# One step for two attention products: the next block's values and the following block's scores are issued together on TensorE, and the values go into the PSUM pair of the next FF1 step

## The chip, the cores and the metric

The kernel runs on one core of one Trainium2 chip. The time is device microseconds of one execution, and the kernel before has a median of 899.84 us over three runs (899.83 to 900.71). Below, TensorE is the matrix engine (PE in the profile, with PEld for its weight loads), VectorE is DVE, ScalarE is ACT, and SyncE (SP) issues the DMAs. PSUM, the memory into which TensorE writes, is used here as four pairs of banks.

## The reference, cut to what matters

Attention inside chunks of 64 rows feeds a feed-forward layer with a rational activation. With 8 batches of 576 tokens there are 4608 tokens, of 8 heads with 64 columns each:

```python
scores = scale * np.matmul(q_c, k_c.transpose(0, 1, 2, 4, 3))
scores = scores - np.max(scores, axis=-1, keepdims=True)
attn = np.exp(scores)
attn = attn / (np.sum(attn, axis=-1, keepdims=True) + 1e-09)
out = np.matmul(attn, v_c)              # x: (4608, 512)
...
h = x @ w_in                            # (4608, 2048)
P = a[0] + a[1] * h + a[2] * h2 + a[3] * h3
Q = 1.0 + np.abs(b[0]) * np.abs(h) + np.abs(b[1]) * h2
g = P / (Q + 1e-06)
return (g @ w_out).astype(np.float32)   # (4608, 512)
```

Everything is float32. The feed-forward products are made from numbers split into a high and a low part, with three products in place of one.

## The kernel before, in words

The tokens are cut into 18 blocks of 256. Each block n has four **stages** s, one for each quarter of the 2048 hidden columns, and a pair (n, s) is a **step** g. Steps 0 to 11 stand in a table written by hand (START) that also splits the weights. From step 12 on, where block 3 begins, a loop writes the steps in one fixed order, and neither a scheduler nor a planner moves anything: the order of the code is the order of each engine's queue. A letter stands for one operation. On TensorE a step holds

- F and f, the first layer (FF1, L332), 48 matmuls of 128x256 into the PSUM tile ph, which lies in the pair p0 or p1 by turns (`ph_tag`);
- Z, z and y, the second layer (FF2, L407) of the step two before (`LAG`), into the pair po, which gathers the four stages of a block.

The rational function of a step runs on ScalarE (a, b and c read ph; I and J, the logarithm and the exponential, follow) and on VectorE (Q; p and P, which read ph; g, H, R, G). FF2 waits for the results of g and G, called ghi and glo. The next FF1 step in the same pair, two steps later, can begin only after P.

The attention of a later block m is laid between these:

- S, the scores (L205, `quarters`): 32 products of 64x64, which the profile shows as 64 matmuls, four at a time in the four quarters of the array, into pss; then M and U on VectorE (maximum, L241 and L249), E on ScalarE (16 exponentials with their sums, L260), n and N on VectorE (L269, L270, L275);
- T, eight transposes on TensorE (L284) into pst, and K, their copy on ScalarE (L288) into at;
- A, the values (L205 again): another 64 such matmuls, into psx; then X on ScalarE and Y on VectorE (L311, L315), which read psx and write the high and low part of the block's x, the input of F.

In the kernel before, pss, pst and psx all take the fourth pair, pa, one after the other. While block n runs, the attention of block m = n + 1 has S, M, U and E in stage 0, n and N in stage 1 with T and K at its end, and A, X and Y in stage 2. Stage 3 holds none of it. The first FF2 matmul after a block of `quarters` is cut at 280 columns instead of 256 (`CUT_FIRST`). SyncE loads q and k of a later block after S, and v after A; its queue also holds the stores of the output, which are issued in stage 1.

Of the kernel before, what the change touches and what calls it, by code (L numbers as in the profile page):

```python
# [19 lines left out]
NB = 18  # L20
# [26 lines left out]
FIRST = 12  # L47
# [7 lines left out]
def tile_chunked_attention_rational_moe(  # L55
# [32 lines left out]
    def bank_pair(tag, name):  # L88
        return ps.tile([P, 2, 512], F32, tag=tag, name=name)
# [4 lines left out]
    def load_qk(n, early=False):  # L94
        if n >= NB:
            return
        if early:
            q, k = (p2.tile([P, W], F32, tag=t, name=f"{t}qk{n}") for t in "AB")
        else:
            qk = p2.tile([P, 2, W], F32, tag="raw", name=f"qk{n}", bufs=3)  # L100
            q, k = qk[:, 0, :], qk[:, 1, :]
        loaded["q", n], loaded["k", n] = q, k
        if not early:
            load_part(n, slice(0, W))

    def load_part(n, c):
        for src, key in ((qT, "q"), (kT, "k")):
            nc.sync.dma_start(out=loaded[key, n][:, c], in_=src[n][:, c])

    def load_v(n):  # L110
        if n >= NB:
            return
        v = p2.tile([P, W], F32, tag="vt", name=f"v{n}", bufs=1)
        nc.sync.dma_start(out=v, in_=vP[n])
        loaded["v", n] = v
# [82 lines left out]
    def quarters(out_cols, tile_out, stat, mov, u):  # L198
        before[0] = "quarters"
        for g in range(NQ)[groups_of(u)]:  # L200
            for par in range(2):
                for c in range(2):
                    rows = slice(64 * c, 64 * c + 64)
                    cols = slice(g * 128 + par * 64, g * 128 + par * 64 + 64)
                    nc.tensor.matmul(  # L205
                        tile_out[par * 64:(par + 1) * 64, c, out_cols(g)],
                        stat[rows, cols], mov[rows, cols], start=True, stop=True,
                    )
# [4 lines left out]
    def have(key, n, make):  # L213
        if (key, n) not in att:
            att[key, n] = make()
        return att[key, n]
# [75 lines left out]
    def att_av(n, u=None, tag="pa"):  # L292
        psx = have("x", n, lambda: bank_pair(tag, f"psx{n}"))

        def cols(g):
            v, hp = divmod(g, NHP)
            return slice(hp * 128 + v * 64, hp * 128 + v * 64 + 64)

        quarters(cols, psx, loaded["v", n], att["at", n], u)
# [116 lines left out]
    def store(n):  # L416
        o = p2.tile([P, 2, DM], F32, tag="eo", name=f"o{n}")
        nc.scalar.copy(o, obuf.pop(n))
        for c in range(2):
            for u in range(UPB):  # L420
                nc.sync.dma_start(out=rows_out(n)[c, u], in_=o[64 * u:64 * u + 64, c, :])
# [3 lines left out]
    def ff2_end(n, s):  # L425
        ghi, glo = gbuf[n, s]
        for i in range(2):
            mm = [(g, w, fi) for g, w in ((ghi, wo_hi), (ghi, wo_lo), (glo, wo_hi)) for fi in range(FPS)]
            for k, (g, w, fi) in enumerate(mm):
                for c in (0, 1):  # L430
                    cols = slice(256 * c, 256 * c + 256)
                    nc.tensor.matmul(  # L432
                        accs[n][i][:, cols], g[:, fi, i * 128:(i + 1) * 128], w[:, FPS * s + fi, cols],
                        start=False, stop=(k == len(mm) - 1 and c == 1),
                    )
            o = p2.tile([P, DM], F32, tag="AB"[i], name=f"oe{i}")
            nc.scalar.copy(o, accs[n][i])
            for u, queue in ((0, nc.sync), (1, nc.scalar)):
                queue.dma_start(out=rows_out(n)[i, u], in_=o[64 * u:64 * u + 64, :])
# [3 lines left out]
    def ph_tag(g):  # L443
        return "p1" if g == 1 or (g >= 10 and g % 2 == 0) else "p0"
# [42 lines left out]
    def run(program, then=""):  # L487
        letters = [item[0] for item in program.split()] + [then]
        for k, item in enumerate(program.split()):
            ahead[0] = next((x for x in letters[k + 1:] if x in "FfZzyr"), "")  # L490
            do[item[0]](*map(int, item[1:].split(".")))
# [4 lines left out]
    total = len(steps)  # L496
    for g in range(FIRST, total + LAG):
        n, s = steps[min(g, total - 1)]
        m, stage = n + 1, s if n + 1 < NB and g < total else None
        one = lambda letters, k: run(" ".join(f"{x}{k}" for x in letters))  # L500
        if g < total:
            one("Ffab", g)
            if stage == 1:
                one("nN", m)
            one("cQ", g)
            if stage == 0:
                one("SMU", m)
                load_qk(m + 1)
            if stage == 2:
                one("A", m)  # L510
                load_v(m + 1)
            one("IJpP", g)
            if stage == 0:
                one("E", m)
            if stage == 2:
                one("X", m)
            one("gHRG", g)
            if stage == 2:
                one("Y", m)
        back = steps[g - LAG]  # L520
        if back == steps[-1]:
            ff2_end(*back)
            continue
        run(" ".join(f"{x}{g - LAG}" for x in "Zzy"), "F" if g + 1 < total else "Z")
        if back[1] == NST - 1:
            store(back[0])
        if stage == 1:
            one("TK", m)


# [34 lines left out]
```

## Time and profile before

| what | value |
|---|---|
| median of three runs | 899.84 us (899.83 to 900.71) |
| span of the profiled execution | 898.1 us |
| around it, to the median of the runs | 1.7 us |
| PE busy | 870.1 us, 97% |
| DVE busy | 748.0 us, 83% |
| ACT busy | 581.9 us, 65% |
| granted TensorE clock, mean | 0.996 |
| FF1 steps (L332) and FF2 (L407 into po) on the chain that ended last | 43% and 42% |
| scores (pss), values (psx), transposes (pst) on that chain | 2%, 2%, 2% |

The span runs from the first to the last instruction of one profiled execution, and the time of a run holds a little more than that. The last two rows are from the chain of waits, followed back from the last instruction. A PE that is 97% busy is not one at its peak, since matmuls are pipelined; how fast they follow each other is read from their starts.

### The profile page before, as it was taken

Reading aid. Unit: us, or ns where it says so; the run is one execution under the profiler, and the core shown is the slowest. Engines: PE = TensorE matmul, PEld = TensorE weight load, DVE = VectorE, ACT = ScalarE, POOL = GpSimd, SP = SyncE. Lnnn points to the kernel's source line nnn. Section 1 sums busy time; section 2 is a strip of 40 time slices with the busy share of each in tenths; the row PEclk is TensorE's granted clock in tenths of the full one; section 3 lists DMA queues with packets and bytes.
Section 4 is the critical chain, followed back from the end, with each engine's and each line's share of the span. In section 5 each row is a group of like instructions: output and inputs, shape, how many; then the busy total and the mean of one; then the engine's idle time right before and its main releaser. Section 6 shows DMA issues by size and latency. Waiting matters only on the chain.

```text
span 898.1 us, 21079 instructions
## 1 busy us (share of the span) xinstructions
PE 870.1 (97%) x9390; PEld 854.2 (95%) x9390; DVE 748.0 (83%) x671; ACT 581.9 (65%) x981; POOL 0.8 (0%) x8
## 2 busy tenths in 40 slices
PE   2699999999999999999999999999999999999998
PEld 2498999999999999999999999999999999999998
DVE  6999997898878878787878897878787878878784
ACT  6899987676656566665747475757565656566452
POOL 0000000000000000000000000000000000000000
PEclk9999999999999999999999999999999999999999
DMA  8525432103030303030201111020202030101010
GB/s 303 213 96 188 168 115 51 69 1 95 2 95 1 95 2 94 1 94 2 65 32 29 68 25 72 17 81 1 95 2 95 1 95 2 48 1 25 1 24 25
DMA packets 16506, 55.88 MB, mean 62 GB/s; under 512 B 2592, under 2 KB 2592, under 8 KB 14368
## 3 DMA queue, kind: packets, MB, share of 16 engines
q1 hardware_dynamic: 16256, 54.28, 18.5%
q8 instruction: 74, 1.21, 0.5%
q10 hardware_dynamic: 160, 0.26, 0.1%
q14 instruction: 16, 0.13, 0.0%
HBM read 45.09 MB, written 9.44 MB: 61 GB/s over the span
## 4 chain that ended last, share of the span: by engine, by line
PE 93%; DVE 3%; DMA 1%; ACT 1%; issue 1%; SPq 0%; ACTq 0%; DVEq 0%
PE ph L332 43%; PE po L407 42%; PE psx L205 2%; PE pss L205 2%; PE pst L284 2%; PE pe L407 1%; DMA Bqk<-in_kT 1%; PE pl L181 1%; DMA raw<-in_w_out 1%; DVE raw L165 0%; PE pe L432 0%; PE po L432 0%; DVE C L360 0%; DVE C L364 0%; DVE raw L161 0%
## 5 line engine op out<-in xcount | busy, mean ns | idle before, releaser
L332 PE MATMUL ph<-xhi,wi_hi 128*128 128x256 f32 x1152 | 322.7, 280 | 6.8 <-DVE C L364 6.8
L332 PE MATMUL ph<-xlo,wi_hi 128*128 128x256 f32 x1152 | 319.8, 278 | 0.0
L332 PE MATMUL ph<-xhi,wi_lo 128*128 128x256 f32 x1152 | 319.5, 277 | 0.0
L337 ACT ACTIVATE A<-ph,ab 128x1024 f32<-128x1024 f32 x72 | 80.7, 1121 | 253.9 <-PE ph L332 253.2
L332 PEld LDWEIGHTS ph<-xhi,wi_hi 128*128 128x128 f32 x1152 | 217.3, 189 | 8.3 <-ACT raw L153 7.5
L407 PE MATMUL po<-wo_hi,ghi 128*128 128x256 f32 (+1 forms) x1112 | 220.4, 280 | 0.0
L332 PEld LDWEIGHTS ph<-xlo,wi_hi 128*128 128x128 f32 x1152 | 217.7, 189 | 0.1
L332 PEld LDWEIGHTS ph<-xhi,wi_lo 128*128 128x128 f32 x1152 | 217.5, 189 | 0.0
L407 PE MATMUL po<-wo_lo,ghi 128*128 128x256 f32 x1112 | 217.1, 276 | 0.0
L348 DVE SCALAR_TENSOR_TENSOR B<-B,ab,A 128x1024 f32<-128x1024 f32 x72 | 92.4, 1283 | 99.0 <-ACT B L340 99.0
L407 PEld LDWEIGHTS po<-wo_hi,ghi 128*128 128x128 f32 x1112 | 167.6, 188 | 2.3 <-issue 0.3
L407 PEld LDWEIGHTS po<-wo_lo,ghi 128*128 128x128 f32 x1112 | 167.6, 188 | 0.0
L407 PE MATMUL po<-wo_hi,glo 128*128 128x256 f32 (+1 forms) x1112 | 138.1, 277 | 0.1
L407 PEld LDWEIGHTS po<-wo_hi,glo 128*128 128x128 f32 x1112 | 131.5, 188 | 0.3 <-DVE glo L381 0.3
L369 DVE SCALAR_TENSOR_TENSOR ghi<-C,ab,A 128x1024 fp32r<-128x1024 f32 x72 | 92.4, 1283 | 10.8 <-ACT A L356 2.4
L352 ACT ACTIVATE A<-B,cst 128x1024 f32<-128x1024 f32 x72 | 83.1, 1155 | 24.8 <-DVE B L348 24.7
L377 DVE SCALAR_TENSOR_TENSOR B<-C,ab,B 128x1024 f32<-128x1024 f32 x72 | 92.3, 1283 | 2.3
L364 DVE SCALAR_TENSOR_TENSOR C<-C,ab,ph 128x1024 f32<-128x1024 f32 x72 | 92.1, 1280 | 2.1
L381 DVE TENSOR_TENSOR glo<-B,A 128x1024 fp32r<-128x1024 f32 x72 | 88.2, 1224 | 6.6
L360 DVE TENSOR_TENSOR C<-C,ph 128x1024 f32<-128x1024 f32 x72 | 87.4, 1214 | 4.2 <-ACT B L340 3.6
L344 ACT ACTIVATE C<-ph,ab 128x1024 f32<-128x1024 f32 x72 | 87.6, 1216 | 4.5 <-PE ph L332 4.5
L373 DVE SCALAR_TENSOR_TENSOR B<-B,ghi 128x1024 f32<-128x1024 f32 x72 | 88.2, 1224 | 2.3
(72 smaller groups left out, 737.3 us busy)
## 6 DMA issues: line engine op xcount, KB each, us to landing
v<-in_vP SPq DMA_DIRECT2D x18, 512.0 KB, 4.1
out<-o SPq DMA_DIRECT2D x68, 128.0 KB, 2.4
raw<-in_w_in SPq DMA_DIRECT2D x8, 1024.0 KB, 6.1
raw<-in_w_out SPq DMA_DIRECT2D x8, 1024.0 KB, 4.8
qk<-in_qT SPq DMA_DIRECT2D x16, 512.0 KB, 4.8
qk<-in_kT SPq DMA_DIRECT2D x16, 512.0 KB, 5.6
Aqk<-in_qT SPq DMA_DIRECT2D x2, 256.0 KB, 5.3
Bqk<-in_kT SPq DMA_DIRECT2D x2, 256.0 KB, 5.8
```

The source lines that it names most:

```text
L332: nc.tensor.matmul(ph[:, fi, :], w[:, cc, f], x[:, cc, :], start=(k == 0), stop=(k == len(mm) - 1))
L337: nc.scalar.activation(ch[n, s][1], ch[n, s][0], AF.Abs, scale=b0)
L344: nc.scalar.activation(ch[n, s][3], ch[n, s][0], AF.Identity, bias=a2, scale=a3)
L348: nc.vector.scalar_tensor_tensor(B, B, b1a, A, ALU.mult, ALU.add)
L352: nc.scalar.activation(A, B, AF.Ln, bias=cst[:, 0:1], scale=2.0 ** -KLN)
L360: nc.vector.tensor_mul(C, C, h)
L364: nc.vector.scalar_tensor_tensor(C, C, a1, h, ALU.add, ALU.mult)
L369: nc.vector.scalar_tensor_tensor(gbuf[n, s][0], C, a0, A, ALU.add, ALU.mult)
L373: nc.vector.scalar_tensor_tensor(B, B, CQ, gbuf[n, s][0].bitcast(F32), ALU.add, ALU.mult)
L377: nc.vector.scalar_tensor_tensor(B, C, a0, B, ALU.add, ALU.subtract)
L381: nc.vector.tensor_mul(gbuf[n, s][1], B, A)
L407: nc.tensor.matmul(accs[n][i][:, cols], g[:, fi, i * 128:(i + 1) * 128], w[:, FPS * s + fi, cols], start=start, stop=stop,)
```

## The change

The loop's order changes, and nothing else does. S of block n + 2 (`early`) is now issued in stage 2 of block n, directly behind A of block n + 1; M, U and E of block n + 2 stand in stage 3, and n and N in stage 0 of the next block. T and K stay at the end of stage 1. A writes into the PSUM pair of the next FF1 step (`ph_tag(g + 1)`) instead of pa. X moves ahead of I on ScalarE, and Y between p and P on VectorE. In stage 2, q and k are loaded right behind v. At step 12 the first S of the loop still stands alone, with M, U, E, n and N where they were; the last A (block 17) stands alone too. Thirteen pairs lie between them (scores of blocks 5 to 17).

```diff
-        m, stage = n + 1, s if n + 1 < NB and g < total else None
+        stage = s if g < total else None
+        m = n + 1 if n + 1 < NB else None
+        early = n + 2 if n + 2 < NB else None
...
             one("Ffab", g)
-            if stage == 1:
+            if stage == 0 and m is not None and g > FIRST:
+                one("nN", m)
+            if g == FIRST + 1:
                 one("nN", m)
             one("cQ", g)
-            if stage == 0:
+            if g == FIRST:
                 one("SMU", m)
                 load_qk(m + 1)
-            if stage == 2:
-                one("A", m)
+            if stage == 3 and early is not None:
+                one("MU", early)
+            if stage == 2 and m is not None:
+                att_av(m, tag=ph_tag(g + 1))
                 load_v(m + 1)
-            one("IJpP", g)
-            if stage == 0:
+                if early is not None:
+                    one("S", early)
+                    load_qk(early + 1)
+                one("X", m)
+            one("Ip", g)
+            if stage == 2 and m is not None:
+                one("Y", m)
+            one("JP", g)
+            if g == FIRST:
                 one("E", m)
-            if stage == 2:
-                one("X", m)
+            if stage == 3 and early is not None:
+                one("E", early)
             one("gHRG", g)
-            if stage == 2:
-                one("Y", m)
...
-        if stage == 1:
+        if stage == 1 and m is not None:
             one("TK", m)
```

TensorE's order from stage 2 of block 4 to stage 0 of block 5, before. The first number in a name is the block: psx5 holds the values of block 5 and pss6 the scores of block 6.

```order
L332 MATMUL ph4_2_2828<-xhi4_2351,wi_lo_68 128x256
L205 MATMUL psx5_2884<-at5_2826,v5_2345 64x64 x32
L407 MATMUL po4_2933<-wo_hi_69,ghi4_0_2640 128x280
...
L332 MATMUL ph5_0_3096<-xhi5_2923,wi_lo_68 128x256
L205 MATMUL pss6_3152<-qk6_2616 64x64 x32
L407 MATMUL po4_2933<-wo_hi_69,ghi4_2_2926 128x280
```

The same place in the changed kernel:

```order
L332 MATMUL ph4_2_2828<-xhi4_2383,wi_lo_68 128x256
L205 MATMUL psx5_2884<-at5_2826,v5_2345 64x64 x32
L205 MATMUL pss6_2919<-qk6_2380 64x64 x32
L407 MATMUL po4_2969<-wo_hi_69,ghi4_0_2643 128x280
...
L332 MATMUL ph5_0_3152<-xhi5_2955,wi_lo_68 128x256
L407 MATMUL po4_2969<-wo_hi_69,ghi4_2_2963 128x256 x2
```

The scores of block 6 have left stage 0 of block 5 and stand behind the values of block 5; FF2 in stage 0 now follows FF1 directly, with the ordinary cut.

ScalarE's order from stage 2 of block 4 on, in the changed kernel (xhi5 is X; the sixteen e6 are E):

```order
L344 ACTIVATE C4_2_2881<-ph4_2_2828,ab_73 128x1024
L311 CAST xhi5_2955<-psx5_2884 128x2x4x128
L352 ACTIVATE A4_2_2877<-B4_2_2878,cst_74 128x1024
L356 ACTIVATE A4_2_2877<-A4_2_2877,cst_74 128x1024
L337 ACTIVATE A4_3_3067<-ph4_3_3018,ab_73 128x1024
...
L356 ACTIVATE A4_3_3067<-A4_3_3067,cst_74 128x1024
L260 ACTIVATE e6_3081,sm6_3074<-pss6_2919,sm6_3074 128x64 x16
L337 ACTIVATE A5_0_3201<-ph5_0_3152,ab_73 128x1024
```

X stood behind L356 of stage 2 and is now ahead of L352; the exponentials of block 6 stood behind L356 of stage 0 of block 5 and now end stage 3 of block 4.

VectorE's order over the same stretch, in the changed kernel (xlo5 is Y; sm6 and e6 are M, U, n and N):

```order
L360 TENSOR_TENSOR C4_2_2881<-C4_2_2881,ph4_2_2828 128x1024
L315 TENSOR_TENSOR xlo5_2956<-psx5_2884,xhi5_2955 128x2x4x128
L364 SCALAR_TENSOR_TENSOR C4_2_2881<-C4_2_2881,ab_73,ph4_2_2828 128x1024
...
L348 SCALAR_TENSOR_TENSOR B4_3_3068<-B4_3_3068,ab_73,A4_3_3067 128x1024
L241 TENSOR_REDUCE sm6_3074<-pss6_2919 128x16
L249 TENSOR_SCALAR sm6_3074<-sm6_3074 128x16
...
L381 TENSOR_TENSOR glo4_3_3099<-B4_3_3068,A4_3_3067 128x1024
L269 TENSOR_SCALAR sm6_3074<-sm6_3074 128x16
L270 RECIPROCAL sm6_3074<-sm6_3074 128x16
L275 TENSOR_TENSOR e6_3081<-e6_3081,sm6_3074 128x2x8x64
L348 SCALAR_TENSOR_TENSOR B5_0_3202<-B5_0_3202,ab_73,A5_0_3201 128x1024
```

Y stood behind L381 of stage 2 and is now ahead of L364; the maximum has moved from stage 0 of block 5 to stage 3 of block 4, and the norm (L275) from ahead of Q (L348) in stage 1 to ahead of Q in stage 0.

## The prediction

> **What bounds the kernel now.** I read the page first: the span, the busy times and the shares of the chain that ended last.
>
> ```profile
> span 898.1 us, 21079 instructions
> ...
> PE 870.1 (97%) x9390; PEld 854.2 (95%) x9390; DVE 748.0 (83%) x671; ACT 581.9 (65%) x981; POOL 0.8 (0%) x8
> ...
> PE 93%; DVE 3%; DMA 1%; ACT 1%; issue 1%; SPq 0%; ACTq 0%; DVEq 0%
> ```
>
> The chain lies on TensorE for 93% of the span. Next, the waits within 210 to 840 us, all that the view lists (engine line, whom it waited for, total us, times, longest):
>
> ```profile
> ACT A L337 <- PE ph L332: 224.3, 53, 5.6
> DVE B L348 <- ACT B L340: 91.5, 54, 2.7
> ACT A L352 <- DVE B L348: 13.8, 54, 0.3
> DVE ghi L369 <- PE pst L284: 0.5, 1, 0.5
> ```
>
> No row has PE as the one that waits: in the loop TensorE goes from one matmul to the next, and the two others wait for it. So the loop's time is the length of TensorE's own stream, and a change is worth what it does to that stream, unless it makes another engine late. The chain in order of time shows one whole round of four steps (start, us, what):
>
> ```profile
> 509.08 5.48 PE ph L332 x48
> 514.56 1.09 PE pss L205 x64
> 515.65 5.66 PE po L407 x48
> 521.31 5.48 PE ph L332 x48
> 526.79 5.45 PE po L407 x48
> 533.11 5.46 PE ph L332 x48
> 538.57 1.09 PE psx L205 x64
> 539.66 5.66 PE po L407 x48
> 545.32 5.48 PE ph L332 x48
> 550.81 5.44 PE po L407 x48
> 556.25 5.48 PE ph L332 x48
> ```
>
> From 509.08 to 556.25 a round takes 47.17 us. Stage 3, which has no attention, takes 556.25 - 545.32 = 10.93; stage 0, with the scores alone, takes 521.31 - 509.08 = 12.23. A block of 64 quarter matmuls standing alone thus costs 1.30 us: 1.09 for itself, and 0.21 because FF2 behind it takes 5.66 instead of 5.45.
>
> **The change on TensorE.** No matmul is added or removed. Scores and values each stood alone between FF1 and FF2, 14 times each in the loop; now 13 pairs stand together, and one scores block (step 12) and one values block (the last) stay alone. What a pair costs depends on what the second block adds behind the first. The timeline of TensorE around the scores (start, us, what; a row holds all that its window touched, so the starts and counts are what to read):
>
> ```profile
> 514.49 1.16 PE L205 MATMUL pss<-qk 64*64 64x64 f32 x64
> ...
> 514.65 1.00 PE L205 MATMUL pss<-qk 64*64 64x64 f32 x56
> ...
> 515.35 0.30 PE L205 MATMUL pss<-qk 64*64 64x64 f32 x8
> ...
> 515.58 0.50 PE L407 MATMUL po<-wo_hi,ghi 128*128 128x280 f32 x2
> ```
>
> From the 56th last at 514.65 to the 8th last at 515.35, 48 matmuls go by in 0.70 us, 14.6 ns each, so 64 in full stream take 0.93 us. The other 1.30 - 0.93 = 0.37 us are edges: getting from matmuls over the whole array to quarters and back. A pair has those edges once. What its inner seam costs no row shows, as no two such blocks now follow each other. Bounds: at least nothing, since the rate inside a block is the fastest seen; at most 0.37, a full set of edges. In between lies 0.16, if the second block takes the whole 1.09 of a lone one and only FF2's excess is saved. The scores' first matmul also carries waits (for its two loads, and for the transposes that had the pair pa), all met long before. The nearest row for a met wait inside a stream that keeps its tile size is FF2's first product with glo, which waits for VectorE:
>
> ```profile
> 506.64 0.39 PE L407 MATMUL po<-wo_hi,ghi 128*128 128x256 f32 x2
> 506.87 0.39 PE L407 MATMUL po<-wo_lo,ghi 128*128 128x256 f32 x2
> ...
> 507.10 1.98 PE L407 MATMUL po<-wo_hi,glo 128*128 128x256 f32 x16
> ```
>
> The step from 506.87 to 507.10 is 0.23, as is the one before it: a met wait costs nothing there. I take a seam of nothing and save 0.37 per pair, **13 x 0.37 = 4.8 us**.
>
> The Trainium skill (TensorEngine Tiling (Array Packing), Key Properties) says that changing the tiling mode drains TensorE while changing only the tile does not. By that rule the seam, 64x64 on both sides, has no drain and the sum stays at 4.8; were each block to drain on entry, it would be 2.7. The trace agrees that the edges cost; that the seam is free no run here shows yet.
>
> **What else moves, and what hides it.** The stream of TensorE stays unbroken only if psx is read before FF1 of stage 3 needs its pair, and if the moved work on ScalarE and VectorE stays ahead of the next reader. Stage 2 of the same round:
>
> ```profile
> 540.53 1.21 ACT L344 ACTIVATE C<-ph,ab 128x1024 f32<-128x1024 f32 x1
> 542.00 1.15 ACT L352 ACTIVATE A<-B,cst 128x1024 f32<-128x1024 f32 x1 [0.26 <-DVE B L348]
> ...
> 544.24 0.99 ACT L311 CAST xhi<-psx 128x1024 fp32r<-128x1024 f32 x1
> ```
>
> ```profile
> 540.67 1.29 DVE L348 SCALAR_TENSOR_TENSOR B<-B,ab,A 128x1024 f32<-128x1024 f32 x1 [2.72 <-ACT B L340]
> 541.88 1.21 DVE L360 TENSOR_TENSOR C<-C,ph 128x1024 f32<-128x1024 f32 x1
> 543.13 1.28 DVE L364 SCALAR_TENSOR_TENSOR C<-C,ab,ph 128x1024 f32<-128x1024 f32 x1
> ...
> 549.65 1.22 DVE L315 TENSOR_TENSOR xlo<-psx,xhi 128x1024 fp32r<-128x1024 f32 x1
> ```
>
> The values are done at 539.66. X (L311) follows c and runs from about 541.74 to 542.73; Y (L315) takes the place of L364 at 543.13 and ends at 544.35. FF1 of stage 3 began at 545.32 and now begins 0.93 later, at 546.25: **1.9 us of slack**. The pair itself is free when the values want it: its last reader is P (L364) of stage 1. In stage 2 P ends at 544.41, 0.9 us ahead of the next FF1, and the values stand behind that FF1, 5.5 us further on. Behind X waits the logarithm (L352), at 542.73 instead of 542.00; with 1.15 and another 1.15 for the exponential it is through at 545.0, before VectorE, which now runs P behind Y until 545.63, asks for it. VectorE's stage ends at 550.87 as before, since Y only changed its place. Were the 1.9 us gone, each further microsecond would cost 14, one for every values block.
>
> The exponentials keep their place in a step but move to one that is followed by a shorter one: from stage 0 with 12.23 us to the next step's ScalarE work, to stage 3 with 10.93. The rows at the end of stage 0 before:
>
> ```profile
> 524.77 0.29 ACT L260 ACTIVATION_READ_ACCUMULATOR e<-pss,sm 128x1 f32 x1
> 526.83 1.12 ACT L337 ACTIVATE A<-ph,ab 128x1024 f32<-128x1024 f32 x1 [1.77 <-PE ph L332]
> ```
>
> ```profile
> 516.66 1.28 DVE L348 SCALAR_TENSOR_TENSOR B<-B,ab,A 128x1024 f32<-128x1024 f32 x1 [1.87 <-ACT B L340]
> ...
> 527.46 1.23 DVE L275 TENSOR_TENSOR e<-e,sm 128x1024 f32<-128x1024 f32 x1
> 528.90 1.28 DVE L348 SCALAR_TENSOR_TENSOR B<-B,ab,A 128x1024 f32<-128x1024 f32 x1 [0.21 <-ACT B L340]
> ```
>
> ScalarE was done 1.77 us before FF1; 1.30 less leaves 0.47, still in time. VectorE, with the norm (L275) ahead of Q, had 0.21 us to spare, so Q of stage 0 now comes 1.30 - 0.21 = 1.1 us late, and with it everything of that step to G. After a plain step of 10.93 it idles 1.87 us (516.66), which takes up the 1.1. The next reader on TensorE is two steps off: FF1 of stage 2 needs P of stage 0. P ends 544.41 - 538.57 = 5.8 us after FF1's end, now 6.9, and that FF1 begins over 16 us after it (one step of 10.93 and an FF2 of 5.45). Nothing on TensorE sees it; cost zero. The softmax has a whole step more before the transposes read it.
>
> On SyncE's queue the order of loads and stores is the same; the loads of q and k are issued two steps earlier, right behind that of v, both behind the end of the values, for which v's buffer waits.
>
> ```profile
> qk<-in_kT SPq DMA_DIRECT2D x16, 512.0 KB, 5.6
> ```
>
> With 5.6 us to land and four steps until the scores read them, they cost nothing even if v's load doubles that.
>
> **Sum.** Against the profiled execution: 898.1 - 4.8 = 893.3 us of span. The median of the runs is 899.84, 1.7 above that span, and this part is untouched: **895.0 us**.
>
> **Rivals.**
>
> 1. *The seam is paid.* The scores' weights cannot be fetched ahead across their waits, or the queue has run dry after 64 such short matmuls, so the second block costs a full 1.09. Then 0.21 per pair is saved: 13 x 0.21 = 2.7, 897.1 us. For it: before a lone block, TensorE does lose time though its waits are met. Against: there the tile size changes too, and at the glo row a met wait cost nothing. The Trainium skill (TensorE: Matmul & The Clock Gate, table at its head) gives a queue of 64 with weight loads pulled ahead of running matmuls; such a queue would hide a short wait, which is against this rival.
> 2. *The change doesn't do what it says.* The seam costs full edges, 0.37; the pairs are no better than two lone blocks, and the time is 899.8, no change. For it: no row shows a seam. Against: 64 quarters in stream show no edge among themselves.
> 3. *Slower: VectorE's delay piles up and FF1 of stage 3 waits for Y.* The 1.1 us of stage 0 are not taken up but carried on, until Y ends after 546.25. It decides from a delay of 1.9 us in stage 2, and makes a loss from 1.9 + 4.8/14 = 2.25. With three delays gathered, 3.3 us, it costs 14 x (3.3 - 1.9) = 20 us less the 4.8 saved: 915 us. For it: VectorE is busy 83% of the span, and stage 0 has no idle time left. Against: the idle times of 1.87 and 2.72 us in other stages.
>
> **How the numbers follow.** The forecast has 0.68 (its own range 894.2 to 896.2, a seam of up to a quarter of the edges or so and the spread of the runs, 0.9 us); the paid seam 0.17; no change 0.08; slower by rival 3 0.07. The range of 8 in 10 goes from 894.0, where the gain is 4.8 and the runs fall low, to 897.4, which takes in the paid seam. A measurement of this kernel can tell about 0.2%, 1.8 us, from no change: both the forecast and rival 1 lie beyond it, so faster has 0.85, the same 0.08, slower 0.07.
>
> **What would show it.** In the profile of the changed kernel the chain of waits should show stage 0 without pss, at 10.93 us, and in stage 2 one piece of 128 quarter matmuls, or two, of 2.0 us together; 2.2 would speak for rival 1, 2.4 for rival 2. In the waits, PE should still not appear in the loop; a row of PE at ph waiting for xlo or xhi would be rival 3. ScalarE's idle time ahead of L337 in stage 0 should shrink to about 0.5, and VectorE's ahead of L348 in stage 0 vanish and come back in stage 1. A round that is shorter by other than 0.37 us, or a gain that stands outside the loop's rounds, would make the working wrong even at the right time.

## The result, and the profile after

The changed kernel has a median of 895.11 us (four runs, 894.77 to 895.22) beside 900.24 us for the kernel before (four runs, 899.83 to 900.71). The ratio is 0.9941, with a 95% interval from 0.9928 to 0.9955: 5.1 us, or 0.6%, faster. The forecast was 895.0 us in a range of 894.0 to 897.4.

The page of the changed kernel, its span, busy times and the shares of the chain that ended last:

```profile
span 893.2 us, 21092 instructions
...
PE 864.7 (97%) x9390; PEld 851.7 (95%) x9390; DVE 745.6 (83%) x671; ACT 580.5 (65%) x981; POOL 0.8 (0%) x8
...
PE 93%; DVE 3%; ACT 1%; DMA 1%; issue 1%; SPq 0%; DVEq 0%; ACTq 0%
```

The span is 4.9 us shorter, with as many matmuls as before. The shares are the same, so the gain is not that another engine got out of the way. The waits of the changed kernel within 210 to 840 us (engine line, whom it waited for, total us, times, longest) are these three and no other:

```profile
ACT A L337 <- PE ph L332: 216.4, 54, 6.9
DVE B L348 <- ACT B L340: 89.9, 41, 3.1
ACT A L352 <- DVE B L348: 23.3, 40, 1.3
```

PE still waits for nobody in the loop. What changed there is that the logarithm (L352) now waits 23.3 us in all instead of 13.8, up to 1.3 instead of 0.3, and that Q (L348) waits 41 times instead of 54. Neither is work that TensorE waits for. The chain of the changed kernel in order of time, one round from FF1 to FF1 (start, us, what):

```profile
530.42 5.46 PE ph L332 x48
535.88 1.09 PE psx L205 x64
536.97 0.93 PE pss L205 x64
537.90 5.66 PE po L407 x48
543.56 5.48 PE ph L332 x48
549.04 5.44 PE po L407 x48
554.49 5.48 PE ph L332 x48
...
565.41 5.48 PE ph L332 x48
...
577.22 5.46 PE ph L332 x48
```

The round takes 577.22 - 530.42 = 46.80 us, 0.37 less than the 47.17 before. The pair is there in two pieces, the values at 1.09 as a lone block had it, and the scores behind them at 0.93, the rate of the full stream; FF2 behind the pair takes 5.66, the 0.21 extra once. Stage 0, from 554.49 to 565.41, takes 10.92 and holds no attention matmul. Thirteen rounds give 13 x 0.37 = 4.8 of the 4.9 us.

The work on ScalarE and VectorE around it, in the timeline of the changed kernel (start, us, engine, line, what, and in brackets the idle time before):

```profile
560.01 1.12 ACT L337 ACTIVATE A<-ph,ab 128x1024 f32<-128x1024 f32 x1 [0.47 <-PE ph L332]
```

```profile
540.31 1.22 DVE L315 TENSOR_TENSOR xlo<-psx,xhi 128x1024 fp32r<-128x1024 f32 x1
...
563.09 1.28 DVE L348 SCALAR_TENSOR_TENSOR B<-B,ab,A 128x1024 f32<-128x1024 f32 x1
...
573.00 1.28 DVE L348 SCALAR_TENSOR_TENSOR B<-B,ab,A 128x1024 f32<-128x1024 f32 x1 [0.85 <-ACT B L340]
```

Y (L315) ends at 541.53, and the FF1 that reads it begins at 543.56 in the chain, which leaves 2.03 us. The timeline has its first matmul at 543.40, 1.87 us behind Y. In stage 0 ScalarE idles 0.47 us ahead of L337, and Q (L348) follows the norm (L275) with no idle time; one step later Q has 0.85 us to spare again.

### The profile page after: what moved, and what is told of

Same layout as the page of the kernel before. It is cut to its first block, busy times and chain, and to the rows that moved or that the text cites. A ratio compares the mean times of both kernels' runs of the same rounds, so it can differ in the third digit from the quotient of the medians.

```text
span 893.2 us, 21092 instructions
## 1 busy us (share of the span) xinstructions
PE 864.7 (97%) x9390; PEld 851.7 (95%) x9390; DVE 745.6 (83%) x671; ACT 580.5 (65%) x981; POOL 0.8 (0%) x8
## 4 chain that ended last, share of the span: by engine, by line
PE 93%; DVE 3%; ACT 1%; DMA 1%; issue 1%; SPq 0%; DVEq 0%; ACTq 0%
PE ph L332 43%; PE po L407 42%; PE psx L205 2%; PE pss L205 2%; PE pst L284 2%; PE pe L407 1%; DMA Bqk<-in_kT 1%; PE pl L181 1%; DVE C L360 0%; DVE raw L165 0%; DVE B L348 0%; PE pe L432 0%; PE po L432 0%; DVE e L275 0%; DVE C L364 0%
## 5 line engine op out<-in xcount | busy, mean ns | idle before, releaser
L337 ACT ACTIVATE A<-ph,ab 128x1024 f32<-128x1024 f32 x72 | 80.7, 1121 | 240.3 <-PE ph L332 239.6
L348 DVE SCALAR_TENSOR_TENSOR B<-B,ab,A 128x1024 f32<-128x1024 f32 x72 | 92.4, 1284 | 97.4 <-ACT B L340 97.4
L352 ACT ACTIVATE A<-B,cst 128x1024 f32<-128x1024 f32 x72 | 83.4, 1158 | 34.3 <-DVE B L348 34.3
L369 DVE SCALAR_TENSOR_TENSOR ghi<-C,ab,A 128x1024 fp32r<-128x1024 f32 x72 | 92.5, 1284 | 10.4 <-ACT A L356 2.4
L381 DVE TENSOR_TENSOR glo<-B,A 128x1024 fp32r<-128x1024 f32 x72 | 88.2, 1225 | 6.6
L364 DVE SCALAR_TENSOR_TENSOR C<-C,ab,ph 128x1024 f32<-128x1024 f32 x72 | 92.1, 1279 | 1.6
```

What stands on the lines that cost most here:

```text
L337: nc.scalar.activation(ch[n, s][1], ch[n, s][0], AF.Abs, scale=b0)
L348: nc.vector.scalar_tensor_tensor(B, B, b1a, A, ALU.mult, ALU.add)
L352: nc.scalar.activation(A, B, AF.Ln, bias=cst[:, 0:1], scale=2.0 ** -KLN)
L364: nc.vector.scalar_tensor_tensor(C, C, a1, h, ALU.add, ALU.mult)
L369: nc.vector.scalar_tensor_tensor(gbuf[n, s][0], C, a0, A, ALU.add, ALU.mult)
L381: nc.vector.tensor_mul(gbuf[n, s][1], B, A)
```

## The experiments

All kernels below are edits of the changed kernel. Where one execution is given, it is compared by its span with the 893.2 us of the changed kernel, whose executions had spans from 893.0 to 893.4; the rows shown recur in the rounds as the text says. None leaves out work; the two with an added matmul write it where the scores overwrite it.

### Does the gain come from the two blocks touching?

My theory was that the whole gain is one set of edges saved per pair. The rival was that it comes from what moved with it: the psx pair, X, Y, the exponentials, the loads. The first kernel keeps all of these and takes only S away from A, into stage 2's FF2, behind its first third.

```diff
                 load_v(m + 1)
-                if early is not None:
-                    one("S", early)
-                    load_qk(early + 1)
...
-        run(" ".join(f"{x}{g - LAG}" for x in "Zzy"), "F" ...)
+        if g < total and stage == 2 and early is not None:
+            run(f"Z{g - LAG} S{early} z{g - LAG} y{g - LAG}", "F")
+            load_qk(early + 1)
+        else:
+            run(" ".join(f"{x}{g - LAG}" for x in "Zzy"), "F" ...)
```

> The changed kernel with one move on TensorE alone: in stage 2 the scores stand behind the first third of FF2 instead of directly behind the values, so the 13 pairs are pulled apart by 32 matmuls; ScalarE, VectorE and the PSUM pairs stay as changed. Theory of the edges (a change from matmuls over the whole array to quarters and back costs 0.37 us each time): 13 more sets of edges, 13 x 0.37 = 4.9 us, back to 900.0 us (the time before). Rival, the gain came from the moved work on ScalarE and VectorE or from the free PSUM pair: it stays at about 895.

It took 911.62 us (910.98 to 912.65), a ratio of 1.0129 to the kernel before (1.0112 to 1.0146), with a span of 909.2: slower than either theory allows. PE waited for nobody here too. The chain of this kernel, part of one round:

```profile
304.83 2.03 PE po L407 x16
306.86 1.09 PE pss L205 x64
307.95 3.97 PE po L407 x32
311.92 5.67 PE ph L332 x48
317.58 5.66 PE po L407 x48
```

The scores alone take 1.09 again, so the edges are back. But FF1 takes 5.67 instead of 5.48 and FF2 5.66 instead of 5.45, and all steps up to the next block of values likewise. One round later they are back at 5.48 and 5.45. The rounds alternate between 47.35 and 48.67 us. TensorE thus streams the same 48 matmuls at two paces, 5.44 / 48 = 113 ns each or 5.66 / 48 = 118 ns, at a full granted clock (it is 1.00 from 503 to 537 us of this run, within a slow round; in the whole run the mean is 0.996, as in the kernel before). Half the rounds at the second pace make 6 or 7 x 1.3 = 8 to 9 us, which hid the answer to the question.

The first matmul behind S is here, as behind every block of quarters, one of 280 columns. The next kernel is the same with that one matmul at 256 columns; behind the values it stays at 280.

```diff
+            run(f"Z{g - LAG} S{early}", "z")
+            before[0] = "ff2"
+            run(f"z{g - LAG} y{g - LAG}", "F")
```

> The kernel with the pairs pulled apart (span 909.2, where 898.1 was expected), with one difference: the FF2 matmul behind the scores is cut at 256 columns instead of 280; the one behind the values keeps 280. In the run before, every second round went at the slow pace from that matmul on (steps of 11.32 in place of 10.93). Theory of the two paces with the cut as the trigger: all rounds fast, only the 13 sets of edges are left, 893.2 + 4.9 = 898.1 of span, 899.9 us. If the trigger is the place (quarters within FF2) and not the cut: some rounds slow again, 905 to 920 of span.

It took 901.49 us (ten runs, 901.05 to 903.02), a ratio of 1.0023 to the kernel before (1.0014 to 1.0033), with a span of 899.9. The chain of this kernel:

```profile
303.23 1.09 PE psx L205 x64
304.32 2.03 PE po L407 x16
306.35 1.09 PE pss L205 x64
307.45 3.96 PE po L407 x32
311.41 5.48 PE ph L332 x48
```

FF1 and all that follows is at 5.48 and 5.44, and each round takes 47.29 us. Values, scores and FF2 together take 1.09 + 2.03 + 1.09 + 3.96 = 8.17 us, against 1.09 + 0.93 + 5.66 = 7.68 in the changed kernel: 0.49 per pair. Of this 0.16 is in the scores (1.09 for 0.93) and 0.33 in FF2. A set of edges is 0.37; the other 0.12 is FF2 behind the scores at the second pace, 32 matmuls that are each some 4 ns longer. With all the other moves in place and only the two blocks pulled apart, nothing of the gain is left. That settles it against the rival.

A third kernel puts S in two halves, behind the first and the second third of FF2, so that a pair becomes three lone blocks.

```diff
+            run(f"Z{g - LAG} S{early}.0 z{g - LAG} S{early}.1 y{g - LAG}", "F")
```

> As the run with the pairs pulled apart, but the scores are also cut in two halves, one behind each third of FF2, so that a block has three short runs of quarters instead of one. Theory of the edges: 26 more sets than the changed kernel, 26 x 0.37 = 9.7 us, 904.8 us; each added set costs the same, whatever the length of the run between them. Rival, the cost goes with the number of quarter matmuls and not with the edges: as the run pulled apart.

It took 905.91 us (905.67 to 906.55), a ratio of 1.0063 (1.0048 to 1.0078). The chain of this kernel:

```profile
305.25 2.03 PE po L407 x16
307.29 0.62 PE pss L205 x32
307.91 2.08 PE po L407 x16
```

Half the scores take 0.62 where 32 quarters in stream would take 0.47, and the third of FF2 behind them takes 2.08 where 16 matmuls in stream take 5.45 / 3 = 1.82. The round is 0.85 us longer than in the changed kernel, 0.42 for each further set of edges. Of this 0.07 is the second pace, since the 16 matmuls behind each half start 118 ns apart in this trace, where those ahead of them start 113 ns apart. What is left, 0.35 for 32 quarters beside 0.37 for 64, is the price of the edges: it doesn't hang on the length of the block.

### What makes an edge: the tile, or the matmul's number format?

In the forecast the seam was free because the tile stays 64x64 on both sides. But the number format stays the same there too: the quarters are float32, and the matmuls of FF1 and FF2 are fp32r. So one matmul over the whole 128x128 array was put into the seam, in one kernel of float32 (a transpose), in the other of fp32r.

```diff
                 if early is not None:
+                    pss = have("s", early, lambda: bank_pair("pa", f"pss{early}"))
+                    nc.tensor.transpose(pss[:, 0, 0:128], ident, ident)
                     one("S", early)
```

> The changed kernel with one extra matmul in each of the 13 seams between values and scores: a 128x128 transpose of the identity in fp32, into the part of PSUM that the scores then overwrite (extra work, not in the reference). It changes the tile size (128x128 between 64x64) but not the number format of the operands. Alone such a transpose goes at 0.10 us. If the edge is the change of tile size: 13 x (0.37 + 0.10) = 6.1 us more, a span of 899.3. If the edge is the change of number format (fp32r to fp32 and back): 13 x 0.10 = 1.3 us, a span of 894.5.

The span was 898.2 us, 5.0 more than the changed kernel's, or 5.0 / 13 = 0.39 per seam, the added matmul's own time included. Its chain:

```profile
538.39 1.09 PE psx L205 x64
539.48 0.26 PE pss L520
539.74 1.09 PE pss L205 x64
```

The scores behind the added matmul take 1.09 instead of 0.93, though the format never changed.

```diff
                 if early is not None:
+                    pss = have("s", early, lambda: bank_pair("pa", f"pss{early}"))
+                    nc.tensor.matmul(pss[:, 0, 0:256], wi_hi[:, 0, 0:P], xbuf[n][0][:, 0, :], ...)
                     one("S", early)
```

> As the run before, but the extra matmul in the seam is one of FF1's kind, 128x128 by 128x256 in fp32r (extra work, overwritten by the scores). It changes both tile size and number format; alone it goes at 0.114 us. Both theories of the edge: a whole set comes back, 13 x (0.37 + 0.11) = 6.3 us more, a span of 899.5. If the edges need a longer run of other matmuls to show (a queue that must run dry first): 13 x 0.11 = 1.5, a span of 894.7.

The span was 899.1 us, 5.9 more, or 0.45 per seam. Its chain:

```profile
540.04 0.31 PE pss L520
540.35 1.09 PE pss L205 x64
```

The one matmul, 0.11 us in stream, stands with 0.31, and the scores with 1.09 again. The rounds of the two kernels take 47.22 and 47.27 us, 0.42 and 0.47 more than those of the changed kernel. About 0.11 of that is the added matmul itself (in stream the transposes T start 109 ns apart and FF1's matmuls 113), so 0.31 and 0.36 of the 0.37 of a set are back. Either format brings most of the cost back; the size of the tile makes the edge. By the rule that the forecast quoted (the Trainium skill, TensorEngine Tiling (Array Packing), Key Properties: a change of mode drains, a change of tile within a mode does not) the trace agrees in both directions: 0.93 without a change of mode, 1.09 with one.

### How far does the cover for Y reach?

Rival 3 was that FF1 comes to wait for Y, decided at 1.9 us of delay and priced at 14 us for each microsecond beyond. Three kernels delay Y by growing amounts. In the first it stands behind P.

```diff
-            one("Ip", g)
+            one("IpJP", g)
             if stage == 2 and m is not None:
                 one("Y", m)
-            one("JP", g)
```

> The changed kernel with Y behind P instead of ahead of it on VectorE; nothing else moves. In the changed kernel Y ends at 541.53 and FF1 of stage 3 begins at 543.40 to 543.56, 2.0 us later. Behind P, Y ends about 1.2 us later: still 0.8 us ahead of FF1. Theory (the pair is given up in time, the slack costs nothing): no change, span 893.2. Rival, the pair already sits at the edge: some us more.

The span was 895.7 us. The thirteen rounds are as long as in the changed kernel, 46.80: 1.28 us of delay are covered. The 2.5 us arise in the last block of values, which has no scores behind it, so that FF1 begins 0.93 earlier. The waits of this kernel there, and its chain:

```profile
PEld ph L332 <- DVE xlo L315: 0.5, 1, 0.5
PE ph L332 <- DVE xlo L315: 0.3, 1, 0.3
```

```profile
823.30 5.92 PE ph L332 x48
829.22 5.66 PE po L407 x48
```

PE waits once for 0.3 us and its weight load (PEld) for 0.5, and every step after that runs at the second pace, 0.2 us longer each, to the end. The forecast's slack of 1.9 us was that of the pairs; the lone values block has 0.93 less, which I did not look at.

In the second kernel Y stands behind g (L369), the first of the four steps from g to G.

```diff
-            one("Ip", g)
-            if stage == 2 and m is not None:
-                one("Y", m)
-            one("JP", g)
+            one("IpJP", g)
...
-            one("gHRG", g)
+            one("g", g)
+            if stage == 2 and m is not None:
+                one("Y", m)
+            one("HRG", g)
```

> The changed kernel with Y one more place back on VectorE, behind the product that makes ghi. Y then ends about 2.6 us later than in the changed kernel, at 544.2, 0.6 us after FF1 of stage 3 could begin. Theory of the slack: FF1 waits for Y in 14 blocks, 0.6 to 0.9 us each, 8 to 13 us more, a span of 901 to 906, and PE shows up in the waits with ph waiting for xlo. If FF1 did not have to wait for the pair: 893.2.

The span was 915.8 us, above what I expected. Two of the waits of this kernel within 210 to 840 us, and two rows of its timeline, one from a round and one from the last values block:

```profile
...
PE ph L332 <- DVE xlo L315: 15.8, 13, 1.2
DVE ghi L369 <- ACT A L356: 6.5, 13, 0.5
```

```profile
506.77 0.35 PE L332 MATMUL ph<-xhi,wi_hi 128*128 128x256 f32 x1 [1.22 <-DVE xlo L315]
...
844.28 0.36 PE L332 MATMUL ph<-xhi,wi_hi 128*128 128x256 f32 x1 [2.15 <-DVE xlo L315]
```

L369 itself waits 0.5 us for ScalarE, so Y comes 1.28 + 1.28 + 0.5 = 3.06 us later than in the changed kernel. FF1's first matmul starts at 506.77, 0.15 us after Y has ended (506.62), where the changed kernel has 1.87 between the two. So 1.87 - 0.15 = 1.72 of the delay are covered and 1.34 are not. PE stood 1.22, and the step grew by 1.37: 13 x 1.37 = 17.8 of the 22.6 us. Another 4.0 came from the last values block: PE stood 2.15 us there, the step grew by 2.3, and then the granted clock fell. The windows of this kernel behind that wait (window, us, busy of PE, PEld, DVE, ACT, POOL, granted clock, DMA share, GB/s):

```profile
844.30:847.60 3.30, 3.30 (x18) 3.30 (x19) 3.16 (x3) 0.00 (x0) 0.00 (x0) 0.60 0.00 0
847.60:851.00 3.40, 3.40 (x29) 3.40 (x29) 0.32 (x1) 0.00 (x0) 0.00 (x0) 0.89 0.02 5
```

A clock of 0.60 over 3.30 us and 0.89 over 3.40 is half the clock for 3.4 us in all, and costs 1.7. In the rounds before, with their waits of 1.2 us, it is 1.00 from 480 to 820 us.

The third kernel has X and Y at their old places, behind P and behind G, with the values still in the next FF1's pair: the cover that the change built is taken away.

```diff
+            one("Ip", g)
+            one("JP", g)
+            if stage == 2 and m is not None:
                 one("X", m)
-            one("Ip", g)
-            if stage == 2 and m is not None:
-                one("Y", m)
-            one("JP", g)
...
             one("gHRG", g)
+            if stage == 2 and m is not None:
+                one("Y", m)
```

> The changed kernel with X and Y at their places before the change, X behind the exponential on ScalarE and Y at the end of VectorE's stage; the values still take the pair of the next FF1 step. Y would end at about 548.1 where the changed kernel's FF1 of stage 3 begins at 543.4: 14 x 4.7 = 66 us more, a span of about 959. From the run with Y behind the product that makes ghi (a wait of 1.4 instead of the 0.6 to 0.9 expected) somewhat more is to be looked for, and where TensorE stands for over 2 us also matmuls at half pace for a while, as in the last block of that run: up to 14 x 6.5 = 91, a span of 984. If the move of X and Y was not needed: 893.2.

The span was 1003.2 us at a mean granted clock of 0.946, 110 us more than the changed kernel's. The wait of PE within 210 to 840 us, and the windows across one of its twelve cases:

```profile
...
PE ph L332 <- DVE xlo L315: 57.0, 12, 4.8
```

```profile
324.50:329.40 4.90, 0.15 (x2) 0.02 (x1) 4.62 (x4) 0.00 (x0) 0.00 (x0) 0.91 0.05 19
329.40:332.80 3.40, 3.39 (x16) 3.40 (x17) 0.00 (x0) 0.00 (x0) 0.00 (x0) 0.50 0.00 0
332.80:336.20 3.40, 3.40 (x21) 3.40 (x21) 0.00 (x0) 0.00 (x0) 0.00 (x0) 0.62 0.00 0
```

PE does almost nothing for 4.90 us while VectorE works off g, H, R, G and Y. Then it is busy throughout, but at half the clock, and 16 and 21 matmuls go by in 3.40 us where 30 would. A clock of 0.91, 0.50 and 0.62 over these windows is half the clock for 0.9 + 3.4 + 2.6 = 6.9 us. The step with the values is 4.92 us longer, and the one after it 2.8: 14 x 7.7 = 108 of the 110 us. The Trainium skill (TensorE: Matmul & The Clock Gate, Part 1) gives half the clock after an idle window of about 3.4 us, with windows that run freely. The 4.9 us here agree. The 2.15 us of the kernel above do not: half the clock followed them too, for a shorter time, so that a wait need not fill 3.4 us for it.

### What sets the second pace?

Several of the kernels above had it, so the changed kernel was run with other sizes of the first matmul behind a block of quarters, which is 256 columns and `CUT_FIRST` more.

```diff
-CUT_FIRST, CUT_LAST = 24, 48
+CUT_FIRST, CUT_LAST = 0, 48
```

> The changed kernel with the first FF2 matmul behind quarters cut at 256 columns as all the others, instead of 280. Theory of the two paces (a run of 128x128 matmuls goes at 113.7 or at 117.8 ns each, set where the run begins behind quarters and kept until the next seam; the odd cut sets the fast one): the slow pace after the quarters, 0.4 us more in each step of 96 matmuls, up to 4 x 0.4 = 1.6 us in each of 14 rounds, a span of 900 to 916. Rival, the cut has nothing to do with the pace: within 1 us of 893.2.

With 256 columns the span was 905.3 us, 12.1 more. The chain of this kernel:

```profile
304.61 0.93 PE pss L205 x64
305.54 5.85 PE po L407 x48
311.39 5.67 PE ph L332 x48
```

The seam of the pair is as good as ever, 0.93. FF2 behind it takes 5.85 instead of 5.66, and in every second round the pace stays for the rest of the round, as in the first kernel.

```diff
-CUT_FIRST, CUT_LAST = 24, 48
+CUT_FIRST, CUT_LAST = 64, 48
```

> The changed kernel with the first FF2 matmul behind quarters cut at 320 columns instead of 280 (256 gave a span of 905.3, with the slow pace in every second round). If a longer first matmul is what sets the fast pace: fast in all rounds as with 280, a span within 1.5 us of 893.2. If 280 is one fitting offset among others that do not fit: slow in some rounds again, 900 to 916.

With 320 columns the span was 896.5 us. The chain of this kernel:

```profile
304.71 5.87 PE po L407 x48
310.58 5.49 PE ph L332 x48
```

```diff
-CUT_FIRST, CUT_LAST = 24, 48
+CUT_FIRST, CUT_LAST = 12, 48
```

> As the run before, with 268 columns, half of the odd cut. If a longer first matmul sets the fast pace and half of it is enough: a span within 1.5 us of 893.2; if it takes the whole 24 columns, slow in some rounds, 900 to 916. No page or run tells which; even chances.

With 268 columns the span was 896.9 us, with FF2 behind the pair at 5.85 and the FF1 behind it at 5.49. In both, FF2 behind the pair has the second pace, and the FF1 behind it ends that: 14 blocks x 0.2 = 2.8 of the 3.3 and 3.7 us. Of the four sizes 280 alone keeps FF2 at the first pace behind the pair. It is no good size as such: in the middle of FF2, behind the scores alone, the second pace followed 280 columns and 256 alike, and in the first experiment, with 280, it went on into FF1 in every second round.

The kernel before shows the second pace as well, ahead of the rounds that the forecast read. The chain of the kernel before, from the end of START to the loop's first step:

```profile
178.49 5.66 PE ph L332 x48
184.15 1.09 PE pss L205 x64
185.25 5.85 PE po L407 x48
191.10 5.49 PE ph L332 x48
```

FF1 goes at the second pace here, and FF2 behind the scores stays at it, though its first matmul has 280 columns. The thirteen traces agree on this: wherever quarters stand between FF1 and FF2, FF2 behind 280 columns has the pace that FF1 had (163 times, 13 of them the second pace), and behind 256, 268 or 320 columns it has the second (45 times, 37 of them behind an FF1 at the first). So 280 columns carry a pace on and do not set it. The pace also changes between FF2 and the FF1 behind it, where the tile size stays the same and PE does not wait: back to the first at 191.10, and from the first to the second at 163.82 in the kernel before. What decides there, and why 280 columns carry the pace, stays open.

## Why the prediction was right

- **What bounds the kernel.** TensorE's stream, with no wait in the loop: so before, and so after. Delays of the other engines changed the time only where a row of PE waiting appeared in the profile.
- **The edges.** A set of 0.37 us, saved 13 times, 4.8 us: the span fell by 4.9, 4.8 of it in the rounds. The kernel with the blocks apart has lost the gain (901.49 us); with three blocks for two each further set costs 0.42, 0.07 of it the second pace.
- **The seam of nothing.** This carried the sum and no row had shown it. The scores behind the values take 0.93, as read off the inside of a block. Rival 1 (1.09 in the seam, 897.1 us) and rival 2 (no gain) are out by this row. The reason is confirmed too: a single matmul over the whole array in the seam makes a round 0.42 or 0.47 longer, only 0.11 of it its own time, whatever its format, though the seam holds the same met waits.
- **What else moves.** ScalarE's idle time ahead of L337 in stage 0 was to fall from 1.77 to 0.47, and is 0.47. Q in stage 0 has none, and 0.85 in the next step; 1.87 - 1.1 = 0.8 follows from the forecast. Slack for Y: 1.9 forecast and 2.03 found, both to the row of the chain where FF1 begins. FF1's first matmul starts 0.16 earlier, and 0.15 behind Y where it has to wait, so the delay that is covered is 1.72.
- **Rival 3** did not happen, and the point from which it decides was about right: 1.28 us of delay cost the rounds nothing, 3.06 cost them 1.37 each. In the rounds a microsecond beyond the cover costs about one, as the forecast had it (1.37 for 1.34). Its price for all of them was mis-sized: "each further microsecond would cost 14" leaves out what a wait can bring with it, the half clock (2.8 us on top of a wait of 4.9, 1.7 on top of one of 2.15) and the second pace (behind the wait of 0.3, not behind those of 1.2). It also counted 14 equal values blocks, where the last one has 0.93 us less slack than the pairs.
- **What the forecast did not say.** It took for granted that FF1 and FF2 keep 5.48 and 5.45 behind the new seam, with `CUT_FIRST` as it was. They do, but they would not have with 256, 268 or 320 columns: 3.3 to 12.1 us, up to more than twice the gain. A rival of that kind, with a price of 0.2 us per step at the second pace, was missing. The trace of the kernel before had rows for it, outside the rounds that the forecast read: FF1 at 5.66 from 178.49, and FF2 behind the scores at 5.85.

## What to carry to other kernels

Where TensorE alone bounds a loop, put blocks of matmuls with the same small tile next to each other: what they cost beyond their stream is paid once per change of tile size (here 0.37 us), and one matmul of the full array between them brings most of it back. Before moving such a block, work out the time by which each reader of its result must be through, in every block and not only the typical one, and keep TensorE from waiting at all: one wait of 0.3 us changed the pace behind it, and one of 2.15 us cost half the clock for 3.4. After any edit at such a seam compare the duration of the plain steps that follow: a stream with the same work and no wait can still run 4% slower.

## What the runs showed of the hardware that I had not expected

- **Two paces of one stream.** 48 matmuls of 128x256 take 5.44 to 5.48 us or 5.66 to 5.67, at a full granted clock and without a wait. The pace changes at a change of tile size, behind a wait, or between FF2 and FF1 with neither, and can last for a round. The eight transposes inside the first experiment's slow round did not end it: the rows on either side of them are 5.65 and 5.66.
- **Half the clock after a short wait.** 2.15 us without matmuls were followed by 3.4 us at half the granted clock, 4.9 us by some 6.9, part of it within the wait; waits of 1.2 us thirteen times over by none.
- **The price of an edge does not scale with the block.** 0.16 us lies in the block of quarters itself, whether it has 64 matmuls (1.09 for 0.93) or 32 (0.62 for 0.47), and 0.19 to 0.21 in the matmuls behind it, the second pace taken off.
